# Top-k attention and channel mix on one core: keys and queries of two heads side by side, all batches in two passes

## The chip, the cores and the metric

The kernel runs on one core of one Trainium2 chip. A time is the device time of that core in microseconds (us) for one launch. Before the change the median of three runs is 1313.34 us (1313.08 to 1314.95).

## The reference

For 8 batches of 8 heads, with 576 positions of 64 features, all in fp32:

```python
scores = scale * np.matmul(q, k.transpose(0, 1, 3, 2))          # per head 576 x 576
kth = np.partition(scores, -32, axis=-1)[..., -32:-31]          # 32nd largest of each row
scores = np.where(scores >= kth, scores, -1e9)
attn = exp(scores - max); attn = attn / (sum(attn) + 1e-9)
x = concatenate_heads(np.matmul(attn, v))                        # per batch 576 x 512
x_prev = x shifted down by one position, zeros first
xk = mu_k * x + (1 - mu_k) * x_prev;  xr the same with mu_r
k = np.maximum(xk @ w_k, 0)                                      # 512 -> 1024
out = sigmoid(xr @ w_r) * (k * k @ w_v)                          # 512 -> 512 and 1024 -> 512
```

## The kernel before

**Attention.** A visit is one batch, one pair of heads and a range of query tiles. A pair of heads has 9 tiles: tiles 0 to 7 are 128 queries of one head (even tiles the first head, odd ones the second), tile 8 holds the last 64 queries of both heads. `EDGE` (line 47) splits batches 0 and 1 into two passes over the pairs (tiles 0 to 3, then 4 to 8) and batch 7 into three; batches 2 to 6 go through each pair in one visit of 9 tiles. That makes 48 visits and 288 tiles.

A visit loads its keys, queries and values by DMA, all issued from SyncE's queue, and turns keys and queries with TensorE transposes (line 833, mode "T") into `rot`, four PSUM banks of 512 columns, from where ScalarE copies them out (line 841). Keys lie as `K[(half, d), head, 288]`: the two halves of the 576 keys stand on the two halves of the 128 partitions, so the queries are loaded and turned twice, once for each half of the partitions. A tile's score (line 880, mode "S") is two matmuls of 64 rows by 288 columns that use the two halves of the array; each is written as two instructions by the build. Tile 8 (line 884, mode "Z") takes four. The 576 scores lie in `ps`, across PSUM banks 0 and 1. ScalarE copies them to `sc` (`keep`, line 889; four buffers), VectorE finds the 24 largest from 7 groups (lines 893 to 898), ScalarE and GpSimd mark what lies below (913, 915), VectorE finds the next 8 and the threshold (916, 918), ScalarE forms the exponentials (921), and VectorE masks them (924). TensorE transposes the masked tile (930; line 939 for the last 64 columns), ScalarE copies it (932, 941), and TensorE multiplies by the values (`weigh`, 961 and 963, mode "W") for two tiles at a time into `sums0` (in bank 0) and `sums1` (in bank 1). The reciprocal of the sums is spread, transposed and copied (`inv`, `inv2`, `spread`, `turni`, `ri`, lines 969 to 997), and `place` (1006) writes the result to `xT`, of which there are two, one for a batch.

**Channel mix.** The 4608 rows go in 19 chunks (`SIZES`, mostly 256). TensorE does it in pieces of mode "R" that `three` (lines 599 to 601) issues: `hidden`, `gate` and `value`, with fp32 split into a high and a low part, three matmuls for one. Their results are in `rot` too. A chunk can begin when all rows that it needs are placed.

**Weights.** 20 blocks of 128 by 512 come as 64-bit numbers and are taken apart (`weight`, lines 1160 to 1185): two ScalarE copies, four VectorE operations (1177 to 1180), one more ScalarE copy, then three GpSimd operations, `wmul`, `wsub` and `wlo` (1183 to 1185). The raw blocks are staged in the space of `hh` and `hl`, and so the first use of `hh` waits for all 20 blocks (`after=X.staged`).

**Order.** The order of every engine's instructions is fixed when the program is built, by a list planner (`Plan.run`). Each operation has a cost, a latency and a key; among those that could start within `NEAR` of the earliest on their engine, the one with the smallest key plus `OFF[name]` goes first. Keys are counted in tiles. TensorE pays for a change of mode (`SWITCH`, `LEAVE`). A wait on another engine adds `WAKE`. PSUM banks are kept exclusive: an operation isn't started while another engine is at work in one of its banks. A mix chunk has the key of its last placed row plus `LAG`, at least `STEP` tiles after the chunk before; a piece may not start until as many scores have been issued as its key plus `PACE` says.

Of the kernel before, what the change touches and what calls it, by code (L numbers as in the profile page):

```python
# [9 lines left out]
F32 = mybir.dt.float32  # L10
# [21 lines left out]
NCH = 7  # L32
# [5 lines left out]
OFF = dict(kt=-7.011, kq=-6.835, rest=-7.805, v=-6.026, v8=-9.812, tk=-4.608, ck=-4.01, tq=-4.295, cq=-5.669, tr=-2.503, cr=-5.25, zero=7.982,  # L38
           score=-0.504, score8=-2.241, keep=-0.323, cand=3.327, best=-1.159, drop=-0.827, under=-0.596, nb=-0.484, count=2.034, below=1.029,
           eighth=2.875, nine=4.624, exps=2.951, mask=3.076, turn=3.921, et=4.228, turnl=3.656, el=1.141, weigh=3.297, inv=-0.082, inv2=5.091,  # L40
           turni=1.833, ri=3.642, place=5.157, lowest=22.268, ranks=1.808, mu=-4.015, nmu=5.336, changek=7.504, sharek=-2.362, addk=-8.89, xhk=-4.232,
           xlk=-11.512, changer=-0.97, sharer=-0.964, addr=4.74, xhr=-2.376, xlr=-5.331, hidden=0.557, relu=-1.816, sq=1.525, r2=-1.905, hl=-3.093,
           gate=2.058, gexp=4.068, ga=2.473, ln=-2.445, inv1=2.025, newton=-3.534, value=0.69, scaled=-3.676, gated=-1.387, store=6.538, w=5.489,
           wabs=-2.2, wclamp=0.087, wshift=-2.193, wsign=0.267, wexp=0.551, wfine=-3.489, whi=1.685, wmul=0.236, wsub=-2.316, wlo=1.183, spread=2.732)
CANDS, BESTS = 0.078, 0.41
# [6 lines left out]
SWITCH = {("T", "T"): 10, ("T", "S"): 92, ("T", "Z"): 92, ("T", "W"): 92, ("T", "R"): -35, ("R", "R"): 85, ("R", "T"): 95, ("R", "S"): 155, ("R", "Z"): 155, ("R", "W"): 185, ("W", "W"): 10}  # L52
BONUS = {("S", "W"): 0.275, ("T", "W"): 0.739, ("R", "W"): 1.45, ("T", "S"): 0.007, ("R", "S"): 0.047, ("W", "S"): -0.327, ("S", "R"): 0.839, ("T", "R"): -0.907, ("W", "R"): -0.036, ("R", "R"): -0.16}
LEAVE = dict(S=95, Z=95, W=103)
SLOW = 1.9
WINDOW, PHASE, WARM, COLD = 3413.0, 2079.0, 0.87, 0.58
NEAR = dict(PE=158, ACT=176, DVE=0, POOL=131, SP=28)
SPREAD, PLACE2 = "POOL", 340
SMALL, BEHIND, JOINT, PEAT = "rot", True, True, 112
# [81 lines left out]
class Plan:  # L141
# [53 lines left out]
    def run(self):  # L195
        lanes = self.LANES
        free = dict.fromkeys(lanes, 0)
# [7 lines left out]
        def base(o):  # L205
            t, w = 0, WAKE[o.lane]
# [9 lines left out]
        def slot_for(b, o):  # L216
# [3 lines left out]
            for i, past in enumerate(b.kind.past):  # L220
                if b.kind.holds[i] is not None:
                    continue
                t = max([0] + [u.end + WAKE[o.lane] for u in past if u.lane != o.lane or u.lane == "SP"])
# [5 lines left out]
        def start(o, t):  # L229
# [7 lines left out]
            for b in o.bufs:  # L237
# [8 lines left out]
                for k in b.kind.banks[slot]:  # L246
                    for lane, end in banks.get(k, {}).items():
                        if lane != o.lane and end + WAKE[o.lane] > t:
                            t = end + WAKE[o.lane]
# [3 lines left out]
        while left:  # L253
# [27 lines left out]
            if lane == "PE":  # L281
                mode = o.mode
                paced += mode in "SZ"
# [34 lines left out]
def topk_attention_channel_mix(ctx: ExitStack, tc: tile.TileContext, q, k, v, mu_k, mu_r, w_k, w_v, w_r, out):  # L318
# [7 lines left out]
    make_identity(nc, ident)  # L326
    ranks_i = consts.tile([128, 9], I32, name="ranks_i")
# [439 lines left out]
    def attend(plan, visits, X, pair_sums):  # L767
# [8 lines left out]
        for p, (b, hp, part) in enumerate(visits):  # L776
# [5 lines left out]
            P.kt = [buf("kt") for _ in range(2)]  # L782
            P.qt = {j: buf("kq") for j in range(2)} if P.first < 8 else {}
            P.K, P.qs = buf("K"), [buf("qs") for _ in P.qt]
# [3 lines left out]
            for j in range(2):  # L788
                def load_k(P=P, b=b, hp=hp, j=j):
                    for i in range(2):  # L790
                        nc.sync.dma_start(P.kt[j].t[:, :, i, :], k[b, 2 * hp + j, i * HS:(i + 1) * HS].rearrange("(b p) d -> p b d", p=KP))
                plan.op(SP, "kt", at0 + 0.01 * j, 1000, 2700, load_k, writes=[P.kt[j]])
            for j in P.qt:
                issue = nc.scalar if soon and j == 0 else nc.sync

                def load_q(P=P, b=b, hp=hp, j=j, c0=c0, nq=nq, issue=issue):
                    for i in range(2):
                        issue.dma_start(P.qt[j].t[:, :nq, i, :], q[b, 2 * hp + j, c0 * 128:(c0 + nq) * 128].rearrange("(c p) d -> p c d", p=128))
                plan.op(ACT if issue is nc.scalar else SP, "kq", at0 + 0.01 * j, 1200, 3000, load_q, writes=[P.qt[j]])
            if full:  # L800
                P.rest, P.qr = buf("rest"), buf("qr")

                def load_r(P=P, b=b, hp=hp):
                    for j in range(2):
                        for i in range(2):
                            nc.sync.dma_start(P.rest.t[j * 64:(j + 1) * 64, 0, i, :], q[b, 2 * hp + j, MAIN:])
# [522 lines left out]
```

## Time and profile before

| | |
|---|---|
| median of 3 runs | 1313.34 us |
| the profiled execution | 1314.63 us, of which the span from first to last instruction is 1312.9 us |
| TensorE busy | 1226.5 us (93%) |
| VectorE busy | 1162.4 us (89%) |
| ScalarE busy | 1135.4 us (86%) |
| GpSimd busy | 1018.3 us (78%) |
| mean granted TensorE clock | 0.967 |

Matmuls are pipelined, so the time that a row's records cover overlaps with the next row; what a visit takes is read from its start to the start of the next row. "Idle before <- X" is the time that the engine stood still, and X what ended it. The granted clock is 1.00 at 2.4 GHz and 0.5 at 1.2 GHz; a number between them is a mean over a stretch.

### The profile page before, as it was taken

The numbers are of one execution on the slowest core, as the hardware profiler recorded it, in microseconds if no ns is written. First come the engines' busy times: TensorE is split into PE (matmuls) and PEld (weight loads), VectorE is DVE, ScalarE is ACT, GpSimd is POOL, SyncE is SP. The second block draws the span as 40 slices with busy tenths as digits, with TensorE's granted clock in tenths as the row PEclk, the third lists the DMA queues.
The fourth block names the chain that finished last, engine by engine and source line by source line (L and its number), as shares of the span: only waits on it lengthen the run. The fifth ranks groups of instructions, "written<-read, shape, count | busy, mean of one in ns | idle before, by whom it ended". The sixth has DMA issues, their size and how long they took to land.

```text
span 1312.9 us, 31609 instructions
## 1 busy us (share of the span) xinstructions
PE 1226.5 (93%) x9685; PEld 930.3 (71%) x9685; DVE 1162.4 (89%) x6222; ACT 1135.4 (86%) x2495; POOL 1018.3 (78%) x908
## 2 busy tenths in 40 slices
PE   7457899999999889999999999999999999999996
PEld 4334667777777567777777777777777787778885
DVE  7999999999999999999999999999999999984011
ACT  7788899999998799999999998999898899896541
POOL 3999986977677388786888787788787787785982
PEclk9576999999999799999999999999999999999998
DMA  6442123222221211212111212111111222222000
GB/s 163 144 126 75 42 56 79 59 66 66 64 50 42 52 42 34 56 34 54 43 49 43 59 42 59 43 49 44 41 32 46 49 66 56 63 53 54 12 25 15
DMA packets 223394, 73.86 MB, mean 56 GB/s; under 512 B 216048, under 2 KB 216048, under 8 KB 223216
## 3 DMA queue, kind: packets, MB, share of 16 engines
q1 hardware_dynamic: 222672, 71.62, 22.2%
q8 instruction: 79, 1.29, 0.4%
q14 instruction: 99, 0.81, 0.2%
q10 hardware_dynamic: 544, 0.13, 0.0%
HBM read 62.26 MB, written 9.44 MB: 55 GB/s over the span
## 4 chain that ended last, share of the span: by engine, by line
PE 42%; DVE 35%; ACT 14%; POOL 5%; issue 3%; DMA 0%; DVEq 0%; SPq 0%; ACTq 0%; POOLq 0%
DVE cand L893 9%; PE rot L599 7%; DVE E L924 7%; PE rot L600 7%; PE rot L601 7%; PE ps L880 6%; DVE top L916 5%; PE ps L961 4%; PE rot L930 4%; DVE top L895 4%; DVE cand L898 4%; ACT sg L913 3%; ACT sc L889 3%; ACT se L921 2%; PE rot L833 2%
## 5 line engine op out<-in xcount | busy, mean ns | idle before, releaser
L915 POOL TENSOR_TENSOR sg<-sc,sg 128x576 f32<-128x576 f32 x288 | 409.9, 1425 | 166.8 <-ACT sg L913 164.8
L893 DVE MAX8 cand<-sc 128x8 f32<-128x82 f32 (+1 forms) x2016 | 397.2, 232 | 6.8 <-ACT sc L889 6.0
L913 ACT ACTIVATE sg<-sc,seen 128x576 f32<-128x576 f32 x288 | 224.1, 778 | 30.7 <-DVE seen L905 28.1
L924 DVE SCALAR_TENSOR_TENSOR E<-sc,seen,se 128x576 f32<-128x576 f32 x288 | 231.2, 803 | 1.3 <-ACT se L921 0.6
L921 ACT ACTIVATE se<-sc,seen 128x576 f32<-128x576 f32 x288 | 215.5, 748 | 13.4 <-DVE E L924 7.0
L916 DVE MAX8 top<-sg 128x8 f32<-128x576 f32 x288 | 215.8, 749 | 4.7 <-POOL sg L915 4.1
L880 PE MATMUL ps<-K,qs 64*128 64x288 f32 x1024 | 203.7, 476 | 14.9 <-ACT sc L889 12.8
L889 ACT ACTIVATE sc<-ps 128x576 f32<-128x576 f32 x288 | 187.1, 650 | 23.8 <-DVE E L924 6.5
L930 PE MATMUL rot<-ident,E 128*128 128x128 f32 x1152 | 184.4, 286 | 4.9 <-DVE E L924 2.2
L895 DVE MAX8 top<-cand 128x8 f32<-128x56 f32 x864 | 180.8, 209 | 7.1 <-DVE rot L969 0.2
L599 PE MATMUL rot<-xh,wk 128*128 128x256 f32 (+2 forms) x608 | 180.8, 297 | 0.0
L932 ACT ACTIVATE et<-rot 128x512 f32<-128x512 f32 x288 | 171.8, 597 | 4.2 <-PE rot L930 3.5
L601 PE MATMUL rot<-xh,wk 128*128 128x256 f32 (+2 forms) x608 | 170.6, 281 | 0.0
L600 PE MATMUL rot<-xl,wk 128*128 128x256 f32 (+2 forms) x608 | 170.5, 280 | 0.0
L930 PEld LDWEIGHTS rot<-ident,E 128*128 128x128 f32 x1152 | 135.2, 145 | 36.5 <-issue 10.4
L961 PE MATMUL ps<-et,v 128*64 128x128 f32 x2048 | 152.5, 290 | 1.1 <-ACT et L932 0.9
L961 PEld LDWEIGHTS ps<-et,v 128*64 128x64 f32 x2048 | 118.6, 143 | 44.1 <-issue 32.1
L880 PEld LDWEIGHTS ps<-K,qs 64*128 64x128 f32 x1024 | 81.0, 194 | 70.7 <-ACT sc L889 26.3
L599 PE MATMUL rot<-wv,hh 128*128 128x512 f32 (+1 forms) x296 | 127.2, 430 | 0.1
L599 PEld LDWEIGHTS rot<-xh,wk 128*128 128x128 f32 x608 | 116.9, 192 | 3.1 <-issue 1.7
L601 PE MATMUL rot<-wv,hl 128*128 128x512 f32 (+1 forms) x296 | 116.9, 395 | 0.0
L600 PE MATMUL rot<-wv,hh 128*128 128x512 f32 (+1 forms) x296 | 116.8, 395 | 0.0
(104 smaller groups left out, 2826.0 us busy)
## 6 DMA issues: line engine op xcount, KB each, us to landing
kt<-in_k SPq DMA_DIRECT2D x192, 72.0 KB, 2.2
v<-in_v SPq DMA_DIRECT2D x92, 128.0 KB, 2.5
kq<-in_q SPq DMA_DIRECT2D x80, 128.0 KB, 2.4
out<-eb SPq DMA_DIRECT2D x35, 256.0 KB, 2.1
kq<-in_q SPq DMA_DIRECT2D x94, 64.0 KB, 2.1
stage<-in_moe_w_k SPq DMA_DIRECT2D x8, 512.0 KB, 4.7
vu<-in_v SPq DMA_DIRECT2D x32, 128.0 KB, 2.3
stage<-in_moe_w_v SPq DMA_DIRECT2D x8, 512.0 KB, 3.7
```

The source lines that it names most:

```text
L599: nc.tensor.matmul(ps, lhsT=sh, rhs=mh, start=first, stop=False)
L600: nc.tensor.matmul(ps, lhsT=sh, rhs=ml, start=False, stop=False)
L601: nc.tensor.matmul(ps, lhsT=sl, rhs=mh, start=False, stop=last)
L880: nc.tensor.matmul(ps.t[:, e * HS:(e + 1) * HS], lhsT=P.qs[j].t[h, c * 128:(c + 1) * 128], rhs=P.K.t[h, j], start=True, stop=True)
L893: lambda T=T, c=c: nc.vector.max(T.cand.t[:, 8 * c:8 * c + 8], T.sc.t[:, CUTS[c]:CUTS[c + 1]]), reads=[T.sc], writes=[(T.cand, c)])
L913: lambda T=T, sn=sn: nc.scalar.activation(T.side.t, T.sc.t, AF.Sign, bias=sn(T, 1), scale=-BELOW, accum_out=T.top.t[:, TOPK:TOPK + 1]),
L915: plan.op(POOL, "below", n, 1375, 1430, lambda T=T: nc.gpsimd.tensor_mul(T.side.t, T.sc.t, T.side.t), reads=[T.sc], writes=[T.side])
L916: plan.op(DVE, "eighth", n, 660, 754, lambda T=T: nc.vector.max(T.top.t[:, 24:32], T.side.t), reads=[T.side], writes=[(T.top, 3)])
L921: plan.op(ACT, "exps", n, 667, 754, lambda T=T, pe=pe, sn=sn: nc.scalar.activation(pe.t, T.sc.t, AF.Exp, bias=sn(T, 0), scale=SCALE), read ...
L924: lambda T=T, U=U, pe=pe, sn=sn: nc.vector.scalar_tensor_tensor(T.e(), T.sc.t, sn(T, 2), pe.t, op0=OP.is_ge, op1=OP.mult, accum_out=U.rs.t ...
L930: nc.tensor.transpose(pt.t[:, c * 128:(c + 1) * 128], E.t[:, o + c * 128:o + (c + 1) * 128], ident)
L961: nc.tensor.matmul(pa[hs[j]], lhsT=vs[j][:, c, :], rhs=ms[c][j], start=(c == 0), stop=False)
```

## The change

**Scores.** One tile `K[(head, d), 512]` holds the first 512 keys of both heads, head by head on the two halves of the partitions; queries lie the same way and are loaded and turned once. One score visit now serves two tiles, one of each head: two matmuls of 64 rows by 512 columns on the two halves of the array, into two banks (`psA`, `psB`). The last 64 keys of both heads stand on the diagonal of `kd`, and one matmul of all 128 rows (`sliver`, planned as mode "T") gives both heads' last 64 columns, into a bank between the two. Tile 8 uses the whole array in mode "Z", which is now planned without a change of mode from "T": 512 columns and twice 64 columns, with queries on the diagonal.

**PSUM.** The scores take three banks (0 to 2) and `rot` three in place of four. The middle bank 1 holds the slivers, `sums0`, `sums1` and a place `last` for the transposes of line 939, which leave `rot`.

**Passes.** Batches 0 to 6 go in two passes, batch 7 in three as before: 68 visits. The values' rests are laid out anew, `vu` is gone.

**Weights.** Only the 8 blocks of `w_k` are staged in `hh` and `hl`; the other 12 in the second `xT`, and batch 1 waits for them there. `w_k` and the rest have starting keys and steps of their own. For blocks 0 to 11 `wsub` and `wlo` become three TensorE matmuls that add and subtract in PSUM, and a ScalarE copy.

**Planner.** `SLACK` is added to `WAKE` in all waits on other engines and banks; all offsets and most constants have other values; `r`, `eb` and `lb` may be given out of turn.

```diff
-EDGE = {0: (range(4), range(4, 9)), 1: (range(4), range(4, 9)), B - 1: (range(4), range(4, 8), range(8, 9))}
-VISITS = [(b, hp, part) for b in range(B) for part in EDGE.get(b, (range(9),)) for hp in range(HP)]
+HALVES = range(4), range(4, 9)
+EDGE = {B - 1: (range(4), range(4, 8), range(8, 9))}
+VISITS = [(b, hp, part) for b in range(B) for part in EDGE.get(b, HALVES) for hp in range(HP)]
-LAG, STEP, WAT, WSTEP, GATE, VALUE, PACE = 10.41, 15.734, 0.542, 1.309, 7.28, 13.747, -2.0
+LAG, STEP, WAT, WSTEP, GATE, VALUE, PACE = 11.185, 15.662, 2.065, 0.589, 7.397, 13.484, -2.0
+SLACK = dict(PE=150, ACT=52, DVE=60, POOL=61)
+LWAT, LWSTEP = 1.027, 1.455
+LAG0, LAG1 = 10.828, 1.959
+WPE = 12
...
+        wake = {lane: WAKE[lane] + SLACK.get(lane, 0) for lane in lanes}
...
-                paced += mode in "SZ"
+                paced += 2 if mode == "S" else mode == "Z"
...
+            def load_k(P=P, b=b, hp=hp):
+                for h in range(2):
+                    nc.sync.dma_start(P.kn.t[:, :, h, :], k[b, 2 * hp + h, :MAIN].rearrange("(c p) d -> p c d", p=128))
...
+            turned(P.kn, 4, "k", lambda P=P: P.K.t, P.K)
+            if P.qn:
+                turned(P.qn, nq, "q", lambda P=P, nq=nq: P.qs.t[:, :nq * 128], P.qs, fast=soon)
+            pt, m = buf("rot"), 1 + full
+            def turn_t(P=P, pt=pt, m=m):
+                for i in range(m):
+                    nc.tensor.transpose(pt.t[:, i * 128:(i + 1) * 128], P.tl.t[:, i * 128:(i + 1) * 128], ident)
...
+                    def score8(P=P, ps=ps, sl=sl):
+                        qd = P.kd.t[:, 128:]
+                        nc.tensor.matmul(ps[0].t, lhsT=qd, rhs=P.K.t, start=True, stop=True)
+                        for h in range(2):
+                            nc.tensor.matmul(sl.t[:, MAIN:S], lhsT=qd, rhs=P.kd.t[:, h * 64:(h + 1) * 64], start=h == 0, stop=h == 1)
...
+                    def sliver(P=P, sl=sl, c=c):
+                        to = sl.t[:, 512:1408].rearrange("p (h x) -> p h x", h=2)[:, :, :64]
+                        nc.tensor.matmul(to, lhsT=P.qs.t[:, c * 128:(c + 1) * 128], rhs=P.kd.t[:, :128].rearrange("p (h x) -> p h x", h=2), start=True, stop=True)
+                    def score(P=P, ps=ps, c=c):
+                        for h in range(2):
+                            w = slice(h * 64, (h + 1) * 64)
+                            nc.tensor.matmul(ps[h].t, lhsT=P.qs.t[w, c * 128:(c + 1) * 128], rhs=P.K.t[w], start=True, stop=True)
...
-                us.add(t // 256)
+                us.add(t // 128)
...
-            r = max(ready[b, u] for b, s, m in pieces for u in units_of(b, s, m)) + LAG
+            r = max(ready[b, u] for b, s, m in pieces for u in units_of(b, s, m)) + min(LAG, LAG0 + c * LAG1)
...
-        key = WAT + n * WSTEP
+        key = WAT + n * WSTEP if name == "k" else LWAT + n * LWSTEP
...
+        if n < WPE:
+            pl = buf("rot")
+            def rest():
+                for i, x in enumerate((val.t, hi, fine.t)):
+                    nc.tensor.matmul(pl.t, lhsT=minus if i == 1 else ident, rhs=x, start=i == 0, stop=i == 2)
+            plan.op(PE_, "wsub", key, 2050, 2250, rest, reads=[val, fine, (W, ('h', which))], writes=[pl], mode="T")
+            done.append(plan.op(ACT, "wlo", key, 520, 630, lambda: nc.scalar.activation(lo, pl.t, AF.Copy), reads=[pl], writes=[(W, which)]))
...
+        made["psA"], made["psB"], made["sl"] = ([a[:, :512]], [(0,)], False), ([a[:, 1024:]], [(2,)], False), ([a], [(1,)], False)
+        made["sums0"], made["sums1"] = ([a[:, 576:704]], [(1,)], False), ([a[:, 704:832]], [(1,)], False)
+        made["last"] = [a[:, 832:960]], [(1,)], False
+        made["rot"] = [pp.tile([128, 512], F32, name=f"rot{i}") for i in range(3)], [(5,), (6,), (7,)], True
```

## Rows read from the trace of the kernel before

**Rows 1.** The page's head and first two parts: busy time, share of the span and instructions of the engines, then busy tenths and the granted clock in 40 slices of 32.8 us.

```profile
span 1312.9 us, 31609 instructions
PE 1226.5 (93%) x9685; PEld 930.3 (71%) x9685; DVE 1162.4 (89%) x6222; ACT 1135.4 (86%) x2495; POOL 1018.3 (78%) x908
...
PE   7457899999999889999999999999999999999996
...
PEclk9576999999999799999999999999999999999998
```

**Rows 2.** Busy time of each engine in seven stretches (columns: start and end, length, PE, weight load, VectorE, ScalarE, GpSimd, each with its count of instructions, then granted clock, DMA share, GB/s).

```profile
0.00:130.40 130.40, 81.49 (x445) 51.08 (x445) 117.95 (x492) 101.50 (x210) 103.84 (x94) 0.76 0.49 128
130.40:164.10 33.70, 28.74 (x254) 23.51 (x255) 31.40 (x174) 27.49 (x63) 30.91 (x27) 0.95 0.18 41
164.10:426.70 262.60, 257.85 (x2128) 193.86 (x2126) 256.83 (x1454) 248.63 (x556) 201.53 (x179) 1.00 0.25 60
426.70:492.30 65.60, 56.53 (x473) 40.55 (x471) 62.83 (x367) 58.25 (x128) 39.43 (x39) 0.90 0.20 47
492.30:1197.00 704.70, 697.49 (x5719) 533.29 (x5717) 681.15 (x3714) 655.57 (x1450) 567.20 (x498) 1.00 0.20 49
1197.00:1290.00 93.00, 92.66 (x618) 78.56 (x614) 10.29 (x22) 40.48 (x85) 69.49 (x68) 1.00 0.08 23
1290.00:1312.90 22.90, 11.70 (x63) 9.43 (x62) 1.97 (x5) 3.47 (x7) 5.91 (x6) 0.83 0.05 16
```

**Rows 3.** ScalarE's copies of scores (line 889) up to the moment when the channel mix begins (ns least, median, greatest, first and last start), and from the timeline of TensorE the first matmul of the mix.

```profile
L889 ACT ACTIVATE sc<-ps x23: 622/646/652, 6.9 to 128.6; 128x576 f32<-128x576 f32 x23
...
130.40 0.39 PE L599 MATMUL rot<-xh,wk 128*128 128x256 f32 x1
```

**Rows 4.** Timeline of TensorE, 425 to 472 us (start, us covered by the records of the row, instruction, count, idle before): the last matmul of one mix chunk and the first of the next, with some of what lies between.

```profile
425.74 0.66 PE L833 MATMUL rot<-ident,kq 128*128 128x128 f32 x4
426.15 0.48 PE L599 MATMUL rot<-wv,hh 128*128 128x512 f32 x1
...
427.40 0.40 PE L601 MATMUL rot<-wv,hl 128*128 128x512 f32 x1
...
432.19 0.66 PE L833 MATMUL rot<-ident,kt 96*128 96x96 f32 x6
432.69 0.28 PE L833 MATMUL rot<-ident,rest 128*128 128x128 f32 x1
...
438.49 0.45 PE L939 MATMUL rot<-ident,E 128*128 128x128 f32 x1 [1.78 <-ACT sg L913]
...
447.75 0.33 PE L988 MATMUL rot<-ident,ri 128*128 128x128 f32 x1 [1.06 <-POOL ri L977]
...
471.79 0.39 PE L599 MATMUL rot<-xh,wk 128*128 128x256 f32 x1
```

**Rows 5.** Timeline of TensorE in the steady part, 703 to 712 us.

```profile
703.17 0.28 PE L600 MATMUL rot<-xl,wk 128*128 128x256 f32 x1
703.29 0.28 PE L601 MATMUL rot<-xh,wk 128*128 128x256 f32 x1
703.50 0.72 PE L884 MATMUL ps<-K,qr 64*64 64x288 f32 x8
704.15 0.33 PE L939 MATMUL rot<-ident,E 128*128 128x128 f32 x1
...
706.25 1.10 PE L961 MATMUL ps<-et,v 128*64 128x128 f32 x16
707.17 0.39 PE L963 MATMUL ps<-el,vr_in 128*64 128x128 f32 x4
...
710.55 0.40 PE L600 MATMUL rot<-wr,xh 128*128 128x512 f32 x1
710.79 0.39 PE L601 MATMUL rot<-wr,xl 128*128 128x512 f32 x1
711.11 0.76 PE L880 MATMUL ps<-K,qs 64*128 64x288 f32 x4
711.80 1.09 PE L961 MATMUL ps<-et,v 128*64 128x128 f32 x16
```

**Rows 6.** Groups of instructions by line and shape: the transposes of keys, queries and the last 64 queries (count, busy us, mean ns).

```profile
L833 PE MATMUL rot<-ident,kq 128*128 128x128 f32 x256 | 48.8, 299 | 0.0
...
L833 PE MATMUL rot<-ident,kt 96*128 96x96 f32 x288 | 42.4, 260 | 4.6 <-DMA kt<-in_k 3.8 <-DVE eb L1179 0.5 <-ACT qs L841 0.2
...
L833 PE MATMUL rot<-ident,rest 128*128 128x128 f32 x32 | 9.3, 289 | 5.9 <-DVE cand L893 5.2 <-issue 0.3 <-ACT sc L889 0.3
```

**Rows 7.** The same view, the staging of the weights on GpSimd, and the instruction of VectorE at line 1180 by itself (ns least, median, greatest, first and last start).

```profile
L1185 POOL TENSOR_TENSOR wk<-eb,lb 128x512 fp32r<-128x512 f32 x8 | 10.4, 1298 | 0.5
L1184 POOL TENSOR_TENSOR eb<-eb,wk 128x512 f32<-128x512 f32 x8 | 10.3, 1290 | 2.0 <-DVE r L1180 1.3 <-ACT wk L1182 0.6
...
L1180 DVE TENSOR_SCALAR r<-eb x20: 409/804/1666, 28.8 to 142.4; 128x512 uint32<-128x512 uint32 x20
```

**Rows 8.** Waits by engine and line, with what they waited for: us in total, times, longest.

```profile
PEld ps L880 <- ACT sc L889: 26.3, 42, 2.6
...
PE ps L880 <- ACT sc L889: 12.8, 21, 2.4
...
ACT sc L889 <- PE ps L963: 6.4, 8, 3.1
```

More of the change, by code (lines that the diff above doesn't have):

```diff
@@ L37 @@
 BIG = 3.0e38
[L38 to L44, printed above, removed]
@@ L45 @@
-CANDS, BESTS = 0.078, 0.41
-LAG, STEP, WAT, WSTEP, GATE, VALUE, PACE = 10.41, 15.734, 0.542, 1.309, 7.28, 13.747, -2.0
-EDGE = {0: (range(4), range(4, 9)), 1: (range(4), range(4, 9)), B - 1: (range(4), range(4, 8), range(8, 9))}
-VISITS = [(b, hp, part) for b in range(B) for part in EDGE.get(b, (range(9),)) for hp in range(HP)]
+OFF = dict(kt=-19.735, kq=-10.45, rest=-15.987, v=-7.343, v8=6.767, tk=-4.984, ck=-3.455, tq=-4.422, cq=-5.589, tr=-1.426, cr=-18.613, zero=19.824,
+           score=-0.387, score8=-6.661, keep=-0.554, cand=4.089, best=-2.373, drop=-6.303, under=-0.607, nb=-1.917, count=2.52, below=2.507,
+           eighth=3.307, nine=6.68, exps=2.93, mask=1.674, turn=3.465, et=4.208, turnl=4.071, el=3.377, weigh=0.847, inv=1.617, inv2=-0.476,
+           turni=-1.478, ri=3.441, place=4.402, lowest=24.856, ranks=-0.087, mu=-14.71, nmu=11.311, changek=11.291, sharek=4.282, addk=-16.721,
+           xhk=-1.799, xlk=-17.496, changer=-4.629, sharer=-0.867, addr=3.883, xhr=-1.605, xlr=-3.824, hidden=2.024, relu=-5.93, sq=2.897, r2=1.674,
+           hl=-2.967, gate=1.931, gexp=3.126, ga=12.306, ln=1.608, inv1=4.333, newton=-9.67, value=1.089, scaled=-10.016, gated=-5.708, store=2.772,
+           w=13.895, wabs=-2.072, wclamp=0.971, wshift=-11.985, wsign=1.043, wexp=-1.834, wfine=-0.159, whi=3.263, wmul=9.248, wsub=-9.325, wlo=1.928,
+           spread=2.307, sliver=-3.433)
@@ L781, in attend @@
             full = part[-1] == 8
[L782 to L784 removed]
+            P.kn, P.tl, P.K, P.kd = buf("kn"), buf("tl"), buf("K"), buf("kd")
+            P.qn, P.qs = (buf("qn"), buf("qs")) if P.first < 8 else (None, None)
             c0 = P.first // 2
@@ L1015, in attend @@
+                    cost = 130 if i == 8 else 64 + 136 * m
+                    plan.op(DVE, "place", n, cost, cost + 90, place, reads=[*U.pa, U.ri], writes=[(xT[b], (hp, U.i // 2 + u)) for u in range(m)], after=X.late if b == 1 else ())
+                    for u in range(m):
+                        ready[b, U.i // 2 + u] = n
             if hp == HP - 1:
@@ L1198, in pipeline @@
         for name, (slots, shape, *dtype) in sizes.items():
-            made[name] = [one.tile(shape, *(dtype or [F32]), name=f"{name}{i}") for i in range(slots)], None, False
+            made[name] = [one.tile(shape, *(dtype or [F32]), name=f"{name}{i}") for i in range(slots)], None, name in ("r", "eb", "lb")
         made["vr"], made["vr8"] = ([vr_hf], None, False), ([vr8_hf], None, False)
@@ L1202, in pipeline @@
         made["wst"] = [t[:, i] for t in stage for i in range(2)], None, False
+        late = made["xT"][0][1].rearrange("p h s -> p (h s)").bitcast(U32)
+        made["wsx"] = [late[:, i * 1024:(i + 1) * 1024].rearrange("p (c t) -> p c t", t=2) for i in range(2)], None, False
+        for t in made["tl"][0]:
+            nc.gpsimd.memset(t, 0.0)
         for name in ("hh", "hl"):
```

236 lines of the change are left out of this document (97 added, 139 removed).

## The prediction

> **What bounds the kernel now.** I read the engines' shares first, then the slices, then windows by stage, then TensorE's timeline where a window stood out. TensorE has the largest share, 93% [rows 1], and the slices show where the missing 7% lie: in the first five, in the two after the thirteenth, and in the last. The windows say the same in us [rows 2]. Up to 130.4 us TensorE works 81.5 and is idle for 48.9; there the channel mix hasn't begun (its first matmul is at 130.4, after 23 copies of scores [rows 3]), and VectorE is busy for 118.0. From 164.1 to 426.7 and from 492.3 to 1197 TensorE is idle for 4.8 of 262.6 and 7.2 of 704.7 us, about 1%; VectorE is at 97%. Between them, 426.7 to 492.3, it is idle for 9.1 us and the clock is 0.90. After 1197 VectorE has almost nothing left (10.3 of 93 us) and TensorE is at 99.6%: a queue of mix work with attention done. So the end is TensorE's: its work, plus its idle time at the start and in the hole at 427. VectorE has 115.9 us to spare behind 1197, ScalarE and GpSimd more. A us that TensorE loses or gains moves the end by one.
>
> **The change part by part**, against the profiled execution's 1314.6 us (1.3 above the median of the runs, 1313.3; the span is 1312.9, with 1.7 around it).
>
> *Scores of tiles 0 to 7.* A visit takes 0.69 us from its start to the next row's (711.11 to 711.80). It starts 0.32 after a matmul that is worth 0.24, so 0.08 to 0.09 goes into entering [rows 5]: 0.78 for a tile, 1.56 for a pair, 128 pairs. The new visit has 512 columns in place of 288. What a column costs: 16 records of the product with the values take 0.92 us (706.25 to 707.17), two halves side by side, two records to a matmul, so 0.23 for 128 columns or 1.8 ns each [rows 5]. New visit: 0.69 + 224 x 1.8 ns = 1.09, plus 0.09 to enter, plus the sliver at 0.23, which has the whole array and no entry of its own: 1.41. Saved: 0.15 x 128 = 19 us. Bounds: if all of the 0.69 grows with the columns, 1.23 + 0.09 + 0.23 = 1.55, and 1 us is saved; with nothing but columns, 0.92 + 0.09 + 0.23 = 1.24, and it is 41. I take 19, since the value product is the same kind of fp32 matmul.
>
> *Tile 8.* Now 0.65 + 0.09 (703.50 to 704.15 [rows 5]). After: 512 + 64 + 64 columns of the whole array, 640 x 1.8 ns = 1.15, with 0.09 to enter from the mix: 1.24. Lost: 0.50 x 32 = 16 us; 13 without an entry, 20 with 0.11 of fixed time on top.
>
> *Turning keys and queries.* Before: 288 transposes of 96 at 0.083 (six in 0.50 [rows 4]) and 256 + 32 of 128 at some 0.105 (four in 0.41; counts and times [rows 4, 6]): 23.9 + 30.2 = 54.1. After: 68 x 4 for keys, 32 x 4 for queries (once, not twice), 68 + 32 for the tails: 500 x 0.105 = 52.5. Two passes cost twenty more key visits, and the single load of queries pays for them: 1.6 saved, 1 taken. ScalarE's copies change as little, and the DMAs, at 20 to 50% of the engines [rows 2], carry 20 more key visits and half the queries: nothing on the path. Loads stay on SyncE's queue, one visit ahead, and a visit is still some 16 us long.
>
> *The hole at 427.* TensorE's last mix matmul starts at 427.40 and the next at 471.79 [rows 4]: 44 us without mix, because chunk 4 holds the first rows of batch 2, and with one pass they are placed only in the last pair's visit. By keys: tile 102 + 10.41 = 112, where the chunk before was due at 80 and a step is 15.7. With two passes the first half of batch 2 is placed at tile 87, and chunk 4 is due at 87 + 11.2 = 98, a step after 81 + 15.7. The last chunk's key comes at 316 in place of 330. What the hole costs [rows 2]: 9.1 us idle less the usual 1% (0.7), and the clock: 0.90 is 6.6 us of full-speed work lost, of which 86% (the busy share) counts, 5.6. Together 14. Bounds: 5 (VectorE is at 96% there too, so part of the idle time may stay) and 15.
>
> *Weights.* `wsub` and `wlo` of 12 blocks leave GpSimd: 12 x (1.29 + 1.30) = 31 us of it [rows 7]. TensorE gets 12 x (2 x 512 x 1.8 ns + 0.24) = 25 us at full clock, up to 50 at the lower level. What hides them is the 48.9 us idle before the mix [rows 2]; behind them in TensorE's order stand scores, and behind those VectorE. If that cover were gone they cost 25. On the other side, the first use of `hh` waits for 8 blocks, not 20, and VectorE's `wexp`, 0.80 at the median and 0.41 at best while GpSimd works beside it [rows 7], may shorten by up to 20 x 0.39 = 8 us; the 5.0 idle of 130 to 164 could go. The first chunk's trigger itself (key 25.8 less 2 in place of 25.4 less 2) stands after the same 24 scores, so the start of the mix hardly moves. Between 25 lost and 12 gained I take 3 gained: GpSimd is no bound of the end, and VectorE sets the pace here.
>
> *PSUM.* `rot` falls from four banks to three; the 160 transposes of line 939 leave it, the mix pieces, `et`, `turni` and the loads stay. Bank 1 gathers sliver, both sums, `last` and both score copies. TensorE's wait on score copies is now 26.3 (at weight loads, mostly hidden) and 12.8 us [rows 8]; the order has 1% of stalls in all. I take 2 lost, between none and the rival below. `SLACK` moves waits further ahead; with 1% of stalls there is little to win, nothing counted.
>
> Of what a shared bank does the rows show this: score copies waited 8 times, 6.4 us, for the products with the values [rows 8], which stand in another part of the same bank. The Trainium skill (PSUM — Partial Sum Buffer, "PSUM bank collisions raise a hardware error") says that two engines may not touch one bank at once, whatever the addresses, and that software has to keep them apart. By the rule the middle bank is one resource for TensorE, ScalarE and VectorE, and by the rows alone it is merely a wait that is seldom seen; the first gives the slower rival, the second the 2 us.
>
> Sum: -19 + 16 - 1 - 14 - 3 + 2 = -19. 1314.6 - 19 = 1295.6, and 1.3 less for the median: 1294. Late next is still TensorE: the tail after attention shrinks from 116 to about 97 us.
>
> **Rivals.**
>
> *Slower: the middle bank.* A score needs both of its pair's copies out of banks 0, 1 and 2; the sliver, the transposes of line 939 and the products stand in TensorE's order behind a bank that ScalarE or VectorE still holds, and mix pieces wait for one of three `rot` banks. Each of the 144 pairs then loses a wait. From 0.13 us a pair (19 / 144) the gain is gone; at 0.3, half of what a wait of a score load on a copy takes now (26.3 / 42 = 0.63 [rows 8]), it is 43 us: 1294 + 41 (43 less the 2 counted) = 1335. For it: three banks and 1% to lose. Against it: such waits are rare now, and `rot` gives up its small users.
>
> *No change: the hole moves.* If the 44 us stay without mix in another place (rows of batch 3, or chunk 1, whose key leaves a gap of 4 tiles), the 14 are not won and the weights bring nothing: 1314.6 - 19 + 16 - 1 + 2 - 1.3 = 1311. For it: VectorE is at 96% in the hole. Against it: by keys every later chunk is due one step after the one before, or less than 4 tiles late.
>
> *Faster: the columns are cheaper and the start shortens.* Score pairs at 1.24 (41 saved in place of 19) with the same hole: 1294 - 22 = 1272. The start at its good end would give 9 more. For it: 0.15 us of the 0.69 has no known cause. Against it: that a change of mode leaves a fixed cost is seen in the 0.09.
>
> **How the numbers follow.** Forecast (1294, own range 1280 to 1307) 0.52; middle bank (1320 to 1350) 0.17; no change (1308 to 1315) 0.11; faster (1265 to 1280) 0.20. A measurement of this kernel tells 0.2%, 2.6 us, from none. Faster by more, below 1310.7: all of the forecast, the faster rival and 0.03 of the third: 0.75. Within: 0.07. Slower: 0.17 and 0.01 of the third: 0.18. The range, 1268 to 1317, leaves out most of the middle bank's case and the end of the faster one.
>
> **What would show it.** Score visits: 128 rows of four records with 512 columns, 1.05 to 1.15 us from start to next, slivers of about 0.23. Tile 8 at 1.2. No stretch over 10 us without mix between 130 and 1197, and a clock of 1.00 all through it. Attention still ends near 1197 (VectorE's work doesn't change), with some 97 us behind it. TensorE's idle time from 164 to 1190 below 1.5%. It is wrong if TensorE's stalls on ScalarE and VectorE in the steady part come to more than 20 us, if the mix starts after 140, if a score pair takes over 1.5 us, or if VectorE ends its attention after 1215.

## The result and the profile after

The changed kernel takes 1326.1 us (median of four runs, 1325.2 to 1327.5), the kernel before 1313.2 beside it: ratio 1.0097, interval 1.0079 to 1.0114. I had forecast 1294 in 1268 to 1317. It is slower, by 13 us, and 32 above my number. The profiled execution took 1327.5, with a span of 1325.7.

The page, its head, shares and slices of 33.1 us:

```profile
span 1325.7 us, 31110 instructions
PE 1237.7 (93%) x9349; PEld 940.2 (71%) x9349; DVE 1152.2 (87%) x6228; ACT 1133.4 (85%) x2491; POOL 985.9 (74%) x885
...
PE   5877899999999999999999999999999999999996
...
PEclk9997999999999999999999999999999999999998
```

TensorE is still the bound, with 11 us more work than before [rows 1]. The two weak slices after the thirteenth are gone: the hole is filled, as predicted. The mix begins where it began:

```profile
130.98 0.44 PE L833 MATMUL rot<-ident,qn 128*128 128x128 f32 x2
131.17 0.36 PE L607 MATMUL rot<-xh,wk 128*128 128x256 f32 x1
```

So the loss lies behind 131. Windows of before, then of after, cut at the first and the last mix matmul (columns as in [rows 2]):

```profile
130.40:1301.30 1170.90, 1144.58 (x9240) 879.12 (x9240) 1042.50 (x5726) 1033.90 (x2286) 914.46 (x815) 0.99 0.20 49
```

```profile
0.00:131.17 131.17, 94.31 (x465) 53.57 (x466) 113.15 (x502) 101.06 (x207) 65.98 (x64) 0.92 0.42 111
131.17:1313.80 1182.63, 1142.95 (x8885) 886.59 (x8884) 1037.08 (x5722) 1032.31 (x2285) 919.87 (x822) 1.00 0.20 49
```

In these stretches TensorE's work, as the view counts it, fell by 1.6 us and its idle time rose from 26.3 to 39.7, though the hole was worth 8.4 of the 26.3 by my reckoning. My sum wanted 9.6 less work (-19 + 16 - 1, and 5.6 by the clock) and 6.4 less idle time (-8.4 + 2). So of the 32 us missed, 20 are stalls and 8 work; 3 are what I had credited to the weights at the start, 1 is the start itself. The line between stalls and work is not sharp: in the run `place_same_order` below, which has the same instructions in the same order, the view counts 8 us more work from the first to the last mix matmul.

Where TensorE stalls is seen by line and shape, within the same stretches (the last columns: idle before the group, and what ended it). Before:

```profile
L880 PE MATMUL ps<-K,qs 64*128 64x288 f32 x932 | 178.5, 460 | 6.2 <-ACT sc L889 5.3 <-DVE xT L1006 0.6
...
L961 PE MATMUL ps<-et,v 128*64 128x128 f32 x1904 | 134.2, 281 | 0.7 <-ACT et L932 0.6
...
L961 PE MATMUL se<-et,v 128*64 128x64 f32 x256 | 21.8, 228 | 3.2 <-DVE seen L905 1.0 <-ACT et L932 0.6 <-ACT r L1110 0.5
```

After:

```profile
L969 PE MATMUL ps<-et,v 128*64 128x128 f32 x1904 | 134.8, 279 | 12.8 <-ACT el L948 11.6 <-ACT et L939 0.5 <-ACT sc L895 0.2
L890 PE MATMUL ps<-K,qs 64*128 64x512 f32 x464 | 131.0, 642 | 2.2 <-ACT el L948 1.5 <-DVE xT L1005 0.6
...
L885 PE MATMUL ps<-kd,qs 128*128 128x128 f32 x232 | 50.4, 299 | 5.5 <-ACT sc L895 4.0 <-DVE cand L900 0.5 <-DVE xT L1005 0.3
...
L969 PE MATMUL ps<-et,v 128*64 128x64 f32 x512 | 21.9, 228 | 2.3 <-ACT el L948 1.4 <-DVE seen L912 0.6
```

The scores and slivers (lines 890 and 885) hardly wait longer, 7.7 for 6.2. The products with the values (line 969, before 961) wait 15.1 us, before 3.9; 13.0 of it is for `el`, the copy of the last 64 keys' transpose (line 948). And what does `el` wait for? Its own line, with what ended ScalarE's idle time:

```profile
L948 ACT ACTIVATE el<-ps x160: 253/277/326, 37.6 to 1239.3; 128x128 f32<-128x128 f32 x160
...
  PE ps L890: 37.2, 51
  PE ps L946: 7.4, 12
```

51 times of 160 it was released not by its own transpose (L946) but by a score (L890) that TensorE runs after that transpose, in other columns of the same tile `ps`, and in banks 0 and 2 where `last` lies in bank 1. In these 51 cases `el` began 1.1 us (median) after the record of its own transpose had ended.

VectorE's last mask starts at 1197.6 before and 1232.9 after, as the least, median, greatest, first and last start of the line show (before, after):

```profile
L924 DVE SCALAR_TENSOR_TENSOR E<-sc,seen,se x288: 789/802/816, 13.9 to 1197.6; 128x576 f32<-128x576 f32 x144
```

```profile
L931 DVE SCALAR_TENSOR_TENSOR E<-sc,seen,se x288: 785/802/817, 25.1 to 1232.9; 128x576 f32<-128x576 f32 x144
```

The work of attention ends 35 us later for a total only 13 longer: the mix ran further ahead (2566 of its 3156 matmuls had begun by 1190 us, before 2508), and less of it is left behind.

### The profile page after: what moved, and what is told of

The parts are those of the page before. It is cut to its first block, busy times and chain, and to the rows that moved or that the text cites. A ratio compares the mean times of both kernels' runs of the same rounds, so it can differ in the third digit from the quotient of the medians.

```text
span 1325.7 us, 31110 instructions
## 1 busy us (share of the span) xinstructions
PE 1237.7 (93%) x9349; PEld 940.2 (71%) x9349; DVE 1152.2 (87%) x6228; ACT 1133.4 (85%) x2491; POOL 985.9 (74%) x885
## 4 chain that ended last, share of the span: by engine, by line
PE 57%; ACT 20%; DVE 14%; POOL 3%; issue 3%; DMA 1%; SPq 1%; ACTq 0%; DVEq 0%; POOLq 0%
PE rot L607 9%; PE rot L609 8%; PE rot L608 8%; PE ps L890 8%; PE ps L969 7%; PE rot L937 6%; ACT sg L920 4%; ACT sc L895 4%; DVE cand L900 3%; ACT et L939 3%; ACT se L928 3%; DVE E L931 2%; PE ps L885 2%; DVE top L923 2%; PE rot L833 2%
## 5 line engine op out<-in xcount | busy, mean ns | idle before, releaser
L900 DVE MAX8 cand<-sc 128x8 f32<-128x82 f32 (+1 forms) x2016 | 377.2, 231 | 23.7 <-ACT sc L895 21.8
L923 DVE MAX8 top<-sg 128x8 f32<-128x576 f32 x288 | 215.9, 750 | 11.6 <-POOL sg L922 10.6
L937 PE MATMUL rot<-ident,E 128*128 128x128 f32 x1152 | 180.9, 281 | 15.7 <-DVE E L931 7.2
L969 PEld LDWEIGHTS ps<-et,v 128*64 128x64 f32 x2560 | 130.9, 138 | 77.1 <-ACT el L948 46.7
L969 PE MATMUL ps<-et,v 128*64 128x128 f32 (+1 forms) x2560 | 169.5, 271 | 15.9 <-ACT el L948 13.7
L937 PEld LDWEIGHTS rot<-ident,E 128*128 128x128 f32 x1152 | 130.0, 141 | 68.6 <-issue 11.4
L890 PE MATMUL ps<-K,qs 64*128 64x512 f32 x512 | 148.3, 657 | 2.2 <-ACT el L948 1.5
L608 PEld LDWEIGHTS rot<-xl,wk 128*128 128x128 f32 x608 | 115.9, 191 | 1.1 <-POOL xl L1092 1.1
```

The costliest lines, as they stand in the source:

```text
L608: nc.tensor.matmul(ps, lhsT=sh, rhs=ml, start=False, stop=False)
L890: nc.tensor.matmul(ps[h].t, lhsT=P.qs.t[w, c * 128:(c + 1) * 128], rhs=P.K.t[w], start=True, stop=True)
L900: lambda T=T, c=c: nc.vector.max(T.cand.t[:, 8 * c:8 * c + 8], T.sc.t[:, CUTS[c]:CUTS[c + 1]]), reads=[T.sc], writes=[(T.cand, c)])
L923: plan.op(DVE, "eighth", n, 660, 754, lambda T=T: nc.vector.max(T.top.t[:, 24:32], T.side.t), reads=[T.side], writes=[(T.top, 3)])
L937: nc.tensor.transpose(pt.t[:, c * 128:(c + 1) * 128], E.t[:, o + c * 128:o + (c + 1) * 128], ident)
L969: nc.tensor.matmul(pa[hs[j]], lhsT=vs[j][:, c, :], rhs=ms[c][j], start=(c == 0), stop=False)
```

## Experiments

The expectations set three theories against each other. W: TensorE loses by waits on the shared places of the middle bank and its tile (`last`, sliver, sums). B: by waits on three rotating banks in place of four. S: by work that I had priced too low. (The expectations of the two runs with one pass have an A and a B of their own, explained there.) All ratios are to the kernel before, run beside it (1312.8 to 1314.6).

**The place of `last`.** First with the order of the plan kept, so that nothing moves but the address:

```
-        made["last"] = [a[:, 832:960]], [(1,)], False
+        made["last"] = [c[:, 896:]], [(1,)], False
```

> The order of every engine is that of the changed kernel; only the place of the transposes of the last 64 columns is another: behind the exponentials instead of the middle bank beside the scores. Theory W (the copy of these columns waits for a score that stands behind its transpose, because both write the tile of the scores, and the product with the values waits for the copy): the wait of this copy on line 890, 37.2 us, goes to nearly 0, TensorE's idle time ahead of the product with the values falls from 15 to about 4, and the time falls by 8 to 14 us, to some 1314, unless the copies now wait for the exponentials or the masks in the same tile. Theory S (the sizes of sliver and tile 8 alone make it slower): the time stays within 3 us of 1326.

1338.9 us, 1.0194 [1.0177, 1.0211]. The wait of `el` for a score is gone, but `se` is the tile of the exponentials, and it is traded for others:

```profile
PEld se L946 <- ACT se L928: 23.8, 42, 2.1
PEld se L946 <- DVE E L931: 22.0, 34, 1.6
...
ACT el L948 <- PE se L946: 20.3, 40, 1.9
```

The new place shares a bank and a tile with the exponentials, which bank 1 did not, and is worse. So theory W's wait is shown to come from the shared tile, but its worth is not told by this run. Then in the rotating banks, as before the change:

```
-LAST, JOINT, PEAT = "last", True, 112
+LAST, JOINT, PEAT = "rot", True, 112
```

> The transposes of the last 64 columns go back to the banks of rot, as before the change; the order is planned anew. Theory W: the copy's wait on scores goes, rot's three banks get 160 more users; net 5 to 12 us faster than the changed kernel. Theory S: within 5 us of 1326. If the three banks of rot are what is short, slower, 1330 or more.

1321.7 us, 1.0056 [1.004, 1.0073]: 4.5 less than the changed kernel. `el` now waits for its transpose alone,

```profile
L948 ACT ACTIVATE el<-rot x160: 254/277/369, 50.1 to 1234.0; 128x128 f32<-128x128 f32 x160
...
  PE rot L946: 7.2, 11
```

and yet, with the mix from 125.1 to 1308.8, TensorE is idle for 36.3 of 1183.7 us: 3.4 less, not the 11 by which the products' wait had grown. Other waits grew, those of the transposes of the masked tile for one:

```profile
L937 PE MATMUL rot<-ident,E 128*128 128x128 f32 x1076 | 169.7, 281 | 8.0 <-ACT el L948 2.0 <-ACT kd L848 1.1 <-DVE E L931 0.9
```

(5.0 in the changed kernel). The mix starts 6 us earlier, but that is not what gained: from 131.2 it stands still for 24.8 us, and by 160 us 48 of its matmuls have begun, in the changed kernel 75. The gain comes behind 160, up to the end of the mix. The changed kernel, then this one:

```profile
160.00:1313.80 1153.80, 1119.25 (x8698) 867.74 (x8697) 1008.77 (x5592) 1006.96 (x2231) 892.39 (x798) 1.00 0.20 48
```

```profile
160.00:1308.80 1148.80, 1121.55 (x8719) 869.82 (x8717) 1004.76 (x5559) 1004.79 (x2225) 885.56 (x793) 1.00 0.20 48
```

34.6 us idle, and now 27.3: 7.3 less, with 2.3 more work. 4.5 lies just under what theory W expected and within what S allowed, so the total does not part them; the idle time speaks for W. Since this kernel has another order, I asked how far any new order moves the time, by a change of one number in the plan:

```
-SLACK = dict(PE=150, ACT=52, DVE=60, POOL=61)
+SLACK = dict(PE=151, ACT=52, DVE=60, POOL=61)
```

> The changed kernel with 151 ns in place of 150 as TensorE's slack in the planner: no instruction is another, only the order is worked out anew. It gives how much a mere new order moves the time, whatever the theory: I expect 1326 within 5 us. If it moves by 10 or more, differences of that size between kernels that are planned anew tell nothing.

1325.7 us, 1.0083 [1.0067, 1.01]: 0.4 below the changed kernel. Its idle time behind 160 is 37.5, 3 more than the changed kernel's. So 4.5 in time and 7.3 in idle time are more than this one new plan did, but of their size I would not be sure to some 3 us.

**The rotating banks.** The kernel before with three:

```
-        made["rot"] = [... for i in range(4)], [(4,), (5,), (6,), (7,)], True
+        made["rot"] = [... for i in range(3)], [(4,), (5,), (6,)], True
```

> The kernel before with three banks for rot in place of four and nothing else (planned anew). If the three banks are what stalls TensorE in the changed kernel (its idle time from 165 to 1193 is 31 us against 21 before, 9 of these in the hole), then 8 to 20 us slower than before, 1321 to 1333. If the banks are not short, within 4 us of 1313.

1341.3 us, 1.0216 [1.0199, 1.0233]: 28 us lost by one bank, more than the 8 to 20 expected, where I had taken 2 for it and the rest of the shared places. The mix starts at 136.5, 6 later, and then takes 20 longer:

```profile
136.50:1327.30 1190.80, 1155.62 (x9227) 878.97 (x9227) 1048.30 (x5690) 1034.26 (x2273) 907.34 (x809) 0.99 0.20 48
```

35.2 of it idle (before 26.3), and 11 more that the view counts as work; 7 of these are the transposes of line 930, from each start to the next one's less idle time 127.8 us in place of 120.8. The hole has little part in it: it is 53 us long for 44, with 9.6 idle (435.9 to 490) for 8.4 (427 to 472). No row shows the missing bank by name: the waits that grew are many and small, as ScalarE's for those transposes, which before is 3.5 us in 7 times:

```profile
ACT et L932 <- PE rot L930: 9.9, 15, 1.4
```

And the changed kernel with two:

```
-        made["rot"] = [... for i in range(3)], [(5,), (6,), (7,)], True
+        made["rot"] = [... for i in range(2)], [(5,), (6,)], True
```

> The changed kernel with two banks for rot in place of three, nothing else (planned anew). Theory B (banks of rot hold TensorE up in the changed kernel as in the kernel before, where the fourth was worth 28 us): the third is worth more than that, 1360 or more. Theory S: under 15 us slower.

1574.7 us, 1.2006 [1.1985, 1.2026]: 249 more than the changed kernel: in this other kernel the next bank costs nine times as much, as theory B had it (1360 or more).

The other direction, more banks, needs room. Here the exponentials move to SBUF, with three banks as a control, with five, and with five and `last` among them:

```
-        c = pp.tile([128, 2 * 512], F32, name="se")
+        c = one.tile([128, S], F32, name="se")
+        rk = one.tile([128, 11], F32, name="rk")
...
-        made["rot"] = [... for i in range(3)], [(5,), (6,), (7,)], True
+        made["rot"] = [... for i in range(5)], [(3,), (4,), (5,), (6,), (7,)], True
```

> The changed kernel with the exponentials (and the ranks) in SBUF in place of PSUM, rot still of three banks; two PSUM banks stand empty. It is the control of the next run. ScalarE writes and VectorE reads another memory, no bank is won: 1326 within 8 us either way.

> The same with the two banks given to rot, which has five. Theory B (three banks for rot in place of four are what costs most: they cost the kernel before 28 us by themselves): 15 to 30 us faster than the control, 1298 to 1312. Theory S (the sizes of sliver and tile 8, 20 us of TensorE's work, decide): within 6 us of the control, since work stays the same.

> Five banks, and the transposes of the last 64 columns in rot as before the change, so that no copy of theirs stands behind a score. By theories B and W together some 4 to 12 us faster than five banks alone, 1290 to 1305; by theory S like the control.

1575.5, 1557.7 and 1545.5 us (1.1997 [1.1975, 1.2019], 1.1855 [1.1835, 1.1875], 1.1765 [1.1745, 1.1784]). The move itself costs 249 us: VectorE becomes the bound (the control's page: 1428.9 busy of 1568.9; the last section says why). The control is as long as the run with two banks, but its bound is another: there VectorE is busy for only 1187.0 of 1572.5. Against that control two more banks give 18 and the place of `last` 12, with the sign that theories B and W gave them, but in a kernel with another bound; they don't price a bank in this one.

**The sizes.** The sliver for one head alone and one product for tile 8's tail:

```
-                        to = sl.t[:, 512:1408].rearrange("p (h x) -> p h x", h=2)[:, :, :64]
-                        nc.tensor.matmul(to, lhsT=..., rhs=P.kd.t[:, :128].rearrange("p (h x) -> p h x", h=2), start=True, stop=True)
+                        to = sl.t[:, 512:576]
+                        nc.tensor.matmul(to, lhsT=..., rhs=P.kd.t[:, :64], start=True, stop=True)
```

> The changed kernel in the same order, with less of TensorE's work: the sliver takes the last 64 keys of the first head alone (64 columns, not 128), tile 8 one product with last keys in place of two. The second head's last 64 scores are left out (zeros), and so are those of tile 8's second head. That takes 128 x 0.12 + 32 x 0.24 = 23 us from TensorE, which is what sliver and tile 8 cost more than the prediction had. Theory S (what decides is TensorE's work, and these two were sized too small): 15 to 23 us faster, 1303 to 1311. Theory W (stalls on the middle bank decide, and TensorE would wait longer instead): under 8 us.

Its total, 4402 us, is no measure: with these scores the kernel's second part ran, which starts over when its test finds a row not settled. In the first part the last mix matmul starts at 1304.7:

```profile
1304.48 0.39 PE L608 MATMUL rot<-wv,hh 128*128 128x512 f32 x1
1304.71 0.39 PE L609 MATMUL rot<-wv,hl 128*128 128x512 f32 x1
```

In the changed kernel it is 1313.45: 8.7 us earlier for about 13 us of work less (slivers 33.2 for 38.8, tile 8 36.2 for 43.8, from start to next less idle time). That is between what theories S (15 or more) and W (under 8) had named. Two thirds of the work saved arrive at the end, so sizes count, though not us for us as the prediction had it; and half the columns save only 14% of a sliver.

**The passes.** The kernel before with two passes for every batch but the last:

```
-EDGE = {0: (range(4), range(4, 9)), 1: (range(4), range(4, 9)), B - 1: ...}
+EDGE = {**{i: (range(4), range(4, 9)) for i in range(B - 1)}, B - 1: ...}
```

> The kernel before, with batches 2 to 6 in two passes too and nothing else changed (planned anew, constants of before). If the hole at 427 us costs what the prediction says, 14 us come back, less 20 more visits' keys at 6 transposes of 0.083 (10 us of TensorE) and their switches: 1305 to 1312, with no stretch of over 10 us without mix and a clock of 1.00 after 165 us. If the hole is worth nothing, 1320 to 1325.

1315.5 us, 1.0013 [1.0003, 1.0022], where 1305 to 1312 had been expected. The hole went (the longest stretch without mix is 7.7 us), TensorE's idle time within the mix fell from 26.3 to 20.6, and nothing was gained: under the old layout keys are turned in more and narrower pieces, and the transposes of line 833, in the profile's busy time,

```profile
L833 PE MATMUL rot<-ident,kt 96*128 96x96 f32 x408 | 59.0, 255 | 5.8 <-DMA kt<-in_k 3.9 <-DVE eb L1179 1.1 <-ACT qs L841 0.5
L833 PE MATMUL rot<-ident,kq 128*128 128x128 f32 x256 | 57.5, 308 | 1.0 <-ACT el L941 0.3 <-ACT ri L993 0.3 <-ACT r L1110 0.2
```

were 42.4 and 48.8 [rows 6]; from start to next, 73.7 became 87.2. Then the reverse, one pass for batches 2 to 6 in the changed kernel, and the same with `last` in the rotating banks:

```
-EDGE = {B - 1: (range(4), range(4, 8), range(8, 9))}
+EDGE = {**{i: (range(9),) for i in range(2, B - 1)}, B - 1: (range(4), range(4, 8), range(8, 9))}
```

> The changed kernel with batches 2 to 6 in one pass again, as in the kernel before (batches 0, 1 and 7 stay as they are, everything else stays changed). Theory A (the two passes buy back the hole of 14 us here too, and cost 20 more visits of keys with 5 transposes of 0.105, 10.5): the hole comes back, 10 of the transposes go: 1326 + 14 - 10 = 1330, with a stretch without mix over 30 us and a clock below 1.00 there. Theory B (the hole's 14 us had already been replaced by stalls on the rotating banks, so filling it bought nothing): the 10 us of transposes come back and no more is lost: 1316, and TensorE's idle time after the start of the mix stays near 44.

> The same, and the place for the transposed last 64 keys is one of the rotating banks, as in the kernel before. Theory A: the 4.5 us that this gave with two passes are had again, 1325.5. Theory B: 1311.5, near the kernel before; if the rotating banks are what is short, though, one pass frees them of 100 transposes, and the gain of the two edits is more than the sum, below 1310.

1338.0 us, 1.0186 [1.0172, 1.02], and 1329.8 us, 1.0123 [1.0108, 1.0139]. Theory B of these two falls, and A is too small: the passes are worth 12 us net here and 8 beside the other edit. The hole is back, 51 us in the first of them and 47 in the second, before 44. One pass, then the changed kernel, in the same 50 us:

```profile
440.00:490.00 50.00, 34.73 (x267) 22.82 (x266) 47.93 (x290) 42.02 (x91) 28.98 (x29) 0.93 0.12 27
```

```profile
440.00:490.00 50.00, 48.04 (x397) 37.54 (x395) 47.26 (x280) 45.95 (x103) 37.91 (x33) 1.00 0.20 47
```

15.3 us idle and a clock of 0.93, against 2.0 and 1.00.

**Weights and slack.** The weights' low parts back on GpSimd; below it, that part alone in the kernel before (with `minus` in the room of the second `xl`), and then with two passes:

```
-WPE = 12
+WPE = 0
```

> The changed kernel with wsub and wlo of all 20 blocks on GpSimd, as before the change (planned anew). The prediction hid these 25 us of TensorE in its idle time ahead of the mix: then 1326 within 5 us. If they delay the start, 5 to 15 us faster; if they keep the start from being GpSimd's, slower.

```
+        if n < WPE:
+            pl = buf("rot")
...
+                for i, x in enumerate((val.t, hi, fine.t)):
+                    nc.tensor.matmul(pl.t, lhsT=X.minus if i == 1 else ident, rhs=x, start=i == 0, stop=i == 2)
```

> The kernel before, where wsub and wlo of blocks 0 to 11 go to TensorE and ScalarE as in the change, and nothing else (planned anew, constants and staging of before, four banks for rot). In the changed kernel undoing this part cost 6 us. If it is a gain by itself, the mix begins some 5 us earlier than 130 and it is 1305 to 1311; if the prediction's 3 us hold, 1308 to 1313; if TensorE's extra 25 us show at all, 1318 or more.

> The same and two passes for batches 0 to 6, with keys and queries as before. Two passes alone cost 2 us. If both parts add up, 1308 to 1315. If, with four banks and the old scores, this is a version that gains from both, below 1305. Theory B says that it is at least 10 us below the changed kernel (1316 or less), since it keeps four banks.

1331.6, 1322.3 and 1315.9 us (1.0129 [1.0108, 1.0149], 1.0079 [1.0058, 1.0099], 1.0023 [1.0011, 1.0036]). Without its weights on TensorE the changed kernel starts its mix at 136.2, 5 later, and ends 5.5 later. In the kernel before they don't lengthen the start (the mix starts at 127.7, and TensorE works 96.8 of the first 130 us at a clock of 0.91, before 81.1 at 0.76), yet the kernel is 9 slower: in the profiled execution its mix takes 8.5 us longer, 6.4 of them idle. With two passes besides, it is 0.5 over the two passes alone. Why 9 in the first case, no run tells.

Slack, added to the planner of the kernel before, and taken from the changed kernel:

```
+        wake = {lane: WAKE[lane] + SLACK.get(lane, 0) for lane in lanes}
...
-                t = max([0] + [u.end + WAKE[o.lane] for u in past if u.lane != o.lane or u.lane == "SP"])
+                t = max([0] + [u.end + wake[o.lane] for u in past if u.lane != o.lane or u.lane == "SP"])
```

> The kernel before with the planner's SLACK of the change and nothing else (planned anew with the constants of before). If planning with later wake-ups costs time itself, because copies and products are put behind other work, 5 to 15 us slower; if it saves stalls, up to 5 faster; the prediction counted it at nothing: within 4 us of 1313.

```
-SLACK = dict(PE=150, ACT=52, DVE=60, POOL=61)
+SLACK = {}
```

> The changed kernel without SLACK in the planner (planned anew, all other constants of the change). If SLACK costs time there, 1310 to 1320; if it does what its name says, the stalls grow and it is 1330 or more; if it does nothing, 1326 within 4.

1316.1 us, 1.0024 [1.0013, 1.0036], and 1340.8 us, 1.0214 [1.0197, 1.0231]. It costs 3 where four banks leave little to wait for, and gives 15 in the changed kernel: without it the mix takes 13 us longer there, 7 of them idle and 6 counted as work. No run beat the kernel before.

## Why the prediction was wrong

*What fell.* Two steps, the price of the lost bank and shared places and the sizes of small matmuls (below). The larger is "I take 2 lost" for the banks. I argued that "`rot` gives up its small users" and that 1% of stalls leaves little room. Taking one bank from the kernel before, which keeps those users, costs 28 (26 between the profiled executions, 6 ahead of the mix and 20 within it). (The changed kernel doesn't start later, but without its weights on TensorE it starts at 136.2, as late as the kernel before with three banks, 136.5.) In the changed kernel the parts are tangled, but those that could be turned one by one can be set side by side: a bank less +28, slack -15, two passes -12, weights -6, together -5. The 13 us lost then leave +18 for the rest, the new scores and the shared places. That is bookkeeping of effects measured in different surroundings, not a proof. The mechanism is that of my slower rival, "the middle bank" with "one of three `rot` banks", priced at 1335 and given 0.17; its point of decision, 0.13 us a pair, was met by 20 us over 144 pairs, 0.14. The rival named the shared bank first, and there it is less right: undoing that alone gave 4.5 of 1326, and 7 of the idle time behind 160, though `el`'s waits vanished. The Trainium skill (Perfetto Trace Analysis, "Matmuls") says that independent groups of matmuls should go round through different PSUM banks, so that emptying one overlaps the next; 28 us for the fourth bank and 249 for the third agree. Where I weighed the rule on one bank's collisions ("one resource for TensorE, ScalarE and VectorE" or "merely a wait that is seldom seen"), the case showed a wider tie than a bank: a copy waits for a later write to another bank of its tile.

*Sizes.* From the timeline's starts, each to the next less idle time, from the first mix matmul on: before, 233 score visits 163.9 us, now 116 pairs 125.5 and their slivers 34.0, so 4.4 less; the mix, whose rows ahead of a score bear the entries (as I read it; no run parts them), 565.3 and now 553.7, 11.6 less. Together -16, where I had -17 for these 116 pairs and part of the 5.6 for the clock: the visit was right (129.92 to 130.98, 1.06, predicted 1.09), the sliver not, 0.29 a pair in place of 0.23. Tile 8, the other term that failed, was 20.5 and is 41.1: +21, not +16. This is its row and that of a pair:

```profile
129.50 0.49 PE L885 MATMUL ps<-kd,qs 128*128 128x128 f32 x2 [0.31 <-ACT sc L895]
129.92 1.13 PE L890 MATMUL ps<-K,qs 64*128 64x512 f32 x4
...
140.43 1.13 PE L875 MATMUL ps<-K,kd 128*128 128x512 f32 x2
141.40 0.55 PE L877 MATMUL ps<-kd 128*128 128x64 f32 x4
141.88 1.09 PE L969 MATMUL ps<-et,v 128*64 128x128 f32 x16
```

0.97 for 512 columns and 0.48 for the two products of 64, where 1.8 ns a column gave 0.92 and 0.23: a product of 64 columns costs about what one of 128 does. I had priced small products by columns alone, from a row of 16 in which they run in pairs on the two halves of the array. These two sizes are the second step that failed: tile 8 took some 5 us and the slivers some 7 (0.06 x 116) more than I had priced. Turning keys and queries I had at -1; it is 58.7 before and 51.7 now, -7, which gives 6 of that back.

*What held.* The hole closed, with a clock of 1.00 throughout, and one_pass shows its worth, 12 net. The start did not move (131.2), and the weights' matmuls (28.6 us from start to next, where I had 25) lay hidden ahead of it; the "3 gained" did not come, though without them 5.5 would be lost. TensorE stayed the bound. Of the marks that I had set for being wrong, two were met: VectorE ends its attention at 1233, past 1215, and TensorE is idle for 31.2 of 1027.3 us in the steady part (165.7 to 1193), 26.6 of it until ScalarE or VectorE released it, past 20; that is 3% where I wanted 1.5. One stretch without mix is a little over my 10 us, 10.4 from 138.9. The slack that I counted at nothing is worth 15; about half of it is idle time of the kind that I had ruled out.

*Open.* How the 20 us of stalls divide: some 7 went when `last` left the shared tile, and how the rest falls to the lost bank and to the other shared places is not shown. All of these kernels but two (`place_same_order` and `shorter_scores`, in the changed kernel's order) were planned anew with the constants of the kernel that they were made from, not with constants fitted to their own banks and passes, so a part of every such difference, of the 28 too, may be the plan's. And no run put back the offsets and other constants that the change altered. A fourth rotating bank in the changed kernel was not tried with its exponentials in PSUM, since the scores take three banks and the exponentials two. The new scores alone, without the lost bank, could not be tried for the same reason.

## To carry to other kernels

A PSUM bank that other stages rotate through has a price even when the profile shows 1% of stalls, since those stalls are few because the bank is there: take it away in the old kernel, one edit and one run, before a change is built on it. Price a small matmul by a row of its own size and mode, not by its columns. And keep apart, as tiles of their own, places that different engines empty at different times, since a copy here waited for a write to another bank of its tile.

## What the hardware showed that I had not expected

With the exponentials in SBUF, the mask of VectorE, which reads two SBUF tiles then, takes up to 2.0 us, and a product of nine elements up to 1.5 (least, median, greatest ns):

```profile
L931 DVE SCALAR_TENSOR_TENSOR E<-sc,seen,se x288: 789/819/2042, 26.0 to 1472.7; 128x576 f32<-128x576 f32 x144
```

```profile
L925 DVE SCALAR_TENSOR_TENSOR nine<-rk,top x288: 199/322/1484, 24.2 to 1471.6; 128x9 f32<-128x9 f32 x144
```

With one of the two in PSUM they take 785 to 817 and 202 to 232. The least times are the same, so the instruction is not slower in itself. What makes it slow is a GpSimd instruction beside it: 54 of these masks had none at any time and took at most 30 ns over the least; of 158 that began while one ran, the median took 0.78 us longer. In the changed kernel 204 began so, and none took over 32 ns longer. With `seen` (line 912, up to 1.35 us in place of 0.16), the three lines took 284 us more, which is all that VectorE's work grew by (277). The Trainium skill (SBUF — State Buffer, "Who interferes with whom") says that a VectorE instruction with two inputs in SBUF contends with a GpSimd instruction that reads SBUF, since its second input comes through a shared read interface; these times agree. The exponentials were in PSUM for more than room.
